# Moving a final check in front of the last products, and one row of outputs in front of the last one

## The chip, the cores and the metric

The kernel runs on one core of a Trainium2 chip. The metric is the device time of one execution in microseconds. The engines are named as the profile names them: PE is TensorE with its matrix products (PEld its weight loads), DVE is VectorE, ACT is ScalarE, POOL is GpSimd and SP is SyncE. An engine's name with a q at its end (DVEq) means its sequencer: semaphore waits, register loads and branches that never reach the engine itself.

## The reference

Routed attention is followed by a two-layer network with an ELU between its layers. A query sees only keys whose nearest centroid is the same as its own:

```python
q_assign = np.argmax(np.einsum('bhsd,hcd->bhsc', q_n, c_n), axis=-1)
k_assign = np.argmax(np.einsum('bhsd,hcd->bhsc', k_n, c_n), axis=-1)
mask = q_assign[:, :, :, None] == k_assign[:, :, None, :]
scores = scale * np.matmul(q, k.transpose(0, 1, 3, 2))
scores = np.where(mask, scores, -1000000000.0)
...
attn = attn / (np.sum(attn, axis=-1, keepdims=True) + 1e-09)
...
h = x @ w_in
g = np.where(h > 0.0, h, alpha * (np.exp(np.minimum(h, 0.0)) - 1.0))
return (g @ w_out).astype(np.float32)
```

There are 4 batches, 8 heads, 768 positions and 64 dimensions per head. The attention output, transposed, is x: 3072 tokens of 512. w_in is 512 x 2048, w_out 2048 x 512. q, k, v and the centroids are float32. The two weight matrices come as float64, and the kernel makes float32 of them during its first part, which the change doesn't touch.

## The kernel before

The work is cut into 48 attention blocks: batch, third of the queries (256 columns), pair of heads. Four of them fill one x of 512 x 256, and each x goes through the network. So there are 12 network blocks, two of them to be done when attention has ended, because the network lags seven attention blocks behind. The order of all instructions is written out by hand in one loop (`for n in range(len(blocks) + LAG)`). Each turn does one attention block, as long as there are any, and one of the four groups of a network block. Each engine takes its own instructions in that order.

A network block has four groups. The first two make the hidden layer (`hidden`, line 491 on PE, exponentials on ACT, clipping on POOL at 502, the ELU on DVE at 508). The third (`first` to `fourth`) and the fourth (`fifth` to `seventh`) make the outputs by a scheme of Strassen's kind: seven products of 8 matmuls (`product`, line 521) into two PSUM banks, `o_bank` and `f_bank`, and additions on ACT, DVE and POOL. In the two blocks behind attention PE has nothing between the products. The additions that matter here are:

- L563 (ACT) copies the third product into the second half of the temporary `ae`.
- L568 (DVE) adds the fourth product to it and writes the first half of the temporary `dt`. Fifth writes the same PSUM bank and so waits for it.
- L574 (DVE) writes the first half of the second output row tile, `o1`, from fifth.
- L581 (DVE) adds the sixth product to that and writes the second half of `o1`; L582 (POOL) then finishes the first half of `o1` with `dt`.
- L587 (DVE) adds the seventh product to the second half of `o1` and writes the second half of the first row tile, `o0`; L588 (POOL) then finishes the second half of `o1` with `ae`, and `store` (L544, on SP's queue) writes both rows of outputs, 256 KB each.

Both temporaries are called `part` in the profile, both output tiles `o_sb`.

At the end (L678 to L687) the kernel asks whether the fast path was allowed: no sum of exponentials or of their reciprocals is over a bound (`r_sum`, `d_sum`, written by ACT in each attention block), and each row has just one nearest centroid (`count`, from DVE). Seven small DVE operations make a flag for each partition (`peak`, `same`, `ok`), a product with a vector of ones adds them up on PE (L686), and a cast makes an integer of it (`go`, L687). Behind `main_path` each engine loads that integer into a register (L55) and branches on it (L56): if it is below 128, the whole computation is done again by `general_path`, and otherwise the engine jumps over that code. With these inputs every engine jumps.

The values of `r_sum`, `d_sum` and `count` are complete when the last attention block is, at n = 48 of the loop.

Of the kernel before, what the change touches and what calls it, by code (L numbers as in the profile page):

```python
# [9 lines left out]
F32 = mybir.dt.float32  # L10
# [4 lines left out]
Alu = mybir.AluOpType  # L15
Axis = mybir.AxisListType
PSUM = bass.MemoryType.PSUM

P = 128
# [6 lines left out]
R_MAX = 1e12  # L26
D_MAX = 1e15
# [33 lines left out]
def main_path(ctx, tc, c, q, k, v, centroids, moe_w_in, moe_w_out, out):  # L61
    nc = tc.nc
    B, H, S, D = q.shape
    NC = centroids.shape[1]
# [3 lines left out]
    HS = S // 2  # L68
    NQ = 3
    QS = S // NQ  # L70
# [8 lines left out]
    const = ctx.enter_context(tc.tile_pool(name="const", bufs=1))  # L79
# [11 lines left out]
    o_bank = long.tile([P, 512], F32, name="o_bank")  # L91
    f_bank = long.tile([P, 512], F32, name="f_bank")

    def banks():
        return short.tile([P, 2, 512], F32, name="banks", tag="banks")
# [13 lines left out]
    def load(name, i):  # L109
        b, pr = pairs[i]  # L110
        src = {"q": q, "k": k, "v": v}[name]
        if (name, i) in staged:
            t = first[:, ts(staged[name, i], 2 * NT * D)]
        elif name == "v":
            t = loads.tile([P, 2 * NT * D], F32, name="v_raw", tag="v", bufs=2)
        else:
            t = loads.tile([P, 2 * NT * D], F32, name=f"{name}_raw", tag="raw", bufs=4)
        if name == "v" or name == "q" and b == 0:
            t = t.rearrange("p (h t d) -> p h t d", h=2, t=NT)
            nc.sync.dma_start(  # L120
                t.rearrange("p h t d -> p h (t d)"),
                src[b, 2 * pr : 2 * pr + 2].rearrange("h (p t) d -> p h (t d)", t=NT),
            )
        elif b == 0:
            t = t.rearrange("p (t h d) -> p t h d", t=NT, h=2)
            for e in range(2):
                nc.sync.dma_start(
                    t[:, :, e], src[b, 2 * pr + e].rearrange("(p t) d -> p t d", t=NT)
                )
        else:  # L130

            for e in range(2):
                for g in range(2):
                    at = 64 * e + 32 * g
                    nc.sync.dma_start(
                        t[at : at + 32].rearrange("p (t a d) -> p t a d", t=NT, d=32),
                        src[b, 2 * pr + e, :, 32 * g : 32 * g + 32].rearrange(
                            "(a p t) d -> p t a d", a=4, t=NT
                        ),
                    )  # L140
        raw[name, i] = t
# [13 lines left out]
    ones = const.tile([P, D], F32, name="ones")  # L155
# [6 lines left out]
    for e in range(2):  # L162
# [4 lines left out]
            axis=Axis.XY,  # L167
            op=Alu.add,
# [27 lines left out]
    count = const.tile([P, 4 * B], F32, name="count")  # L196
    r_sum = const.tile([P, NQ * len(pairs)], F32, name="r_sum")
    d_sum = const.tile([P, NQ * len(pairs)], F32, name="d_sum")
# [92 lines left out]
    def w_parts():  # L291
        e_, f_ = w_out[:, : FC // 2, :QS], w_out[:, : FC // 2, QS:]
        g_, h_ = w_out[:, FC // 2 :, :QS], w_out[:, FC // 2 :, QS:]
        return e_, f_, g_, h_
# [98 lines left out]
    blocks = [(b, third, pr) for b in range(B) for third in range(NQ) for pr in range(NPR)]  # L393
# [125 lines left out]
    def product(to, left, right):  # L519
        for f in range(FC // 2):  # L520
            nc.tensor.matmul(  # L521
                to[:, :QS],
                lhsT=left[:, f],
                rhs=right[:, f],
                start=(f == 0),
                stop=(f == FC // 2 - 1),
            )

    def outer(b, third):
        half = FC // 2  # L530
        a_, c_ = g[:, :half, :P], g[:, :half, P:]
        b_, d_ = g[:, half:, :P], g[:, half:, P:]
        e_, f_, g_, h_ = w_parts()
        t1, t2, t4 = (w_sum[:, n] for n in range(3))
        seen = {}

        def temp():
            return loads.tile([P, 2, QS], F32, name="part", tag="ex", bufs=3)

        def out_tile():  # L540
            return work.tile([P, DM], F32, name="o_sb", tag="o_sb")

        def store(m, o_sb):
            nc.sync.dma_start(  # L544
                out[b * S : (b + 1) * S].rearrange("(p t) m -> p t m", t=NT)[:, QT * third + m],
                o_sb,
            )

        def first():
            product(o_bank, a_, e_)  # L550
            seen["ae"] = temp()
            nc.scalar.copy(seen["ae"][:, 0], o_bank[:, :QS])
            nc.vector.tensor_tensor(a_, g_sum, a_, op=Alu.add)

        def second():
            product(f_bank, b_, g_)
            o0, _ = seen["o"] = out_tile(), out_tile()
            nc.vector.tensor_tensor(o0[:, :QS], f_bank[:, :QS], seen["ae"][:, 0], op=Alu.add)
            nc.vector.tensor_tensor(b_, b_, g_sum, op=Alu.subtract)

        def third_():
            product(o_bank, c_, f_)
            nc.scalar.copy(seen["ae"][:, 1], o_bank[:, :QS])  # L563

        def fourth():
            product(f_bank, d_, t4)
            seen["dt"] = temp()
            nc.vector.tensor_tensor(  # L568
                seen["dt"][:, 0], f_bank[:, :QS], seen["ae"][:, 1], op=Alu.add
            )  # L570

        def fifth():
            product(f_bank, g_sum, t2)
            nc.vector.tensor_tensor(  # L574
                seen["o"][1][:, :QS], f_bank[:, :QS], seen["ae"][:, 0], op=Alu.add
            )

        def sixth():
            product(o_bank, a_, t1)
            o = seen["o"][1]  # L580
            nc.vector.tensor_tensor(o[:, QS:], o_bank[:, :QS], o[:, :QS], op=Alu.add)  # L581
            nc.gpsimd.tensor_tensor(o[:, :QS], o[:, :QS], seen["dt"][:, 0], op=Alu.add)  # L582

        def seventh():
            product(f_bank, b_, h_)
            o0, o1 = seen["o"]
            nc.vector.tensor_tensor(o0[:, QS:], f_bank[:, :QS], o1[:, QS:], op=Alu.add)  # L587
            nc.gpsimd.tensor_tensor(o1[:, QS:], o1[:, QS:], seen["ae"][:, 1], op=Alu.add)  # L588
            store(0, o0)
            store(1, o1)  # L590

        return [first, second, third_, fourth], [fifth, sixth, seventh]

    def mlp(b, third):

        steps = [lambda n=n: hidden(b, third, n) for n in range(FC // 4)]
        yield steps[:2]
        yield steps[2:] + [finish]
        yield from outer(b, third)
# [8 lines left out]
    def load_v(n):  # L608
        b, third, pr = blocks[n]
        if n not in seen:  # L610
            seen.add(n)
            load("v", b * NPR + pr)
            raw["v", n] = raw.pop(("v", b * NPR + pr))

    seen = {0}
    raw["v", 0] = raw.pop(("v", 0))
# [9 lines left out]
    for n in range(len(blocks) + LAG):  # L626
# [8 lines left out]
        if n + 1 < len(blocks):  # L635
            load_v(n + 1)
# [34 lines left out]
        for other in beside[done:]:  # L671
            if other:
                other()

    ok = c["ok"]
    peak = const.tile([P, 2], F32, name="peak")
    same = const.tile([P, 4 * B], F32, name="same")
    nc.vector.tensor_reduce(peak[:, 0:1], r_sum, axis=Axis.X, op=Alu.add)  # L678
    nc.vector.tensor_reduce(peak[:, 1:2], d_sum, axis=Axis.X, op=Alu.add)
    nc.vector.tensor_scalar(ok[:, 0:1], peak[:, 0:1], R_MAX, None, op0=Alu.is_lt)  # L680
    nc.vector.tensor_scalar(ok[:, 1:2], peak[:, 1:2], D_MAX, None, op0=Alu.is_lt)
    nc.vector.tensor_scalar(same, count, float(HS // NC), None, op0=Alu.is_equal)
    nc.vector.tensor_reduce(ok[:, 2:3], same, axis=Axis.X, op=Alu.min)
    nc.vector.tensor_reduce(ok[:, 3:4], ok[:, 0:3], axis=Axis.X, op=Alu.min)
    ps = banks()[:, 0]
    nc.tensor.matmul(ps[:1, :1], lhsT=ok[:, 3:4], rhs=ones[:, :1], start=True, stop=True)  # L686
    nc.vector.tensor_copy(c["go"], ps[:1, :1])  # L687


@with_exitstack  # L690
# [251 lines left out]
```

## Time and profile before

| what | us |
|---|---|
| median of 5 runs (1040.69 to 1043.05) | 1041.84 |
| profiled execution | 1041.97 |
| its span, first to last instruction | 1039.8 |
| around the span | 2.17 |
| PE busy | 1004.4 (97%) |
| DVE busy | 515.9 (50%) |
| ACT busy | 343.5 (33%) |
| POOL busy | 115.7 (11%) |
| mean DMA rate | 53 GB/s |

The granted clock of PE was 0.993 over the span. DVE, ACT and POOL wait for PE most of the time: their idle time costs nothing by itself. What counts is when PE waits, and what is left to do after its last product. A line of a timeline gives the start, the busy time, the engine, the line of the kernel, the operation with the tiles that it writes and reads, the shape, the number of instructions and, in brackets, how long the engine had been idle and who released it. A product of 8 matmuls shows as x16, because each float32 matmul takes two passes.

### The profile page before, as it was taken

Reading aid. Unit: us, or ns where it says so; the run is one execution under the profiler, and the core shown is the slowest. Engines: PE = TensorE matmul, PEld = TensorE weight load, DVE = VectorE, ACT = ScalarE, POOL = GpSimd, SP = SyncE. Lnnn points to the kernel's source line nnn. Section 1 sums busy time; section 2 is a strip of 40 time slices with the busy share of each in tenths; the row PEclk is TensorE's granted clock in tenths of the full one; section 3 lists DMA queues with packets and bytes.
Section 4 is the critical chain, followed back from the end, with each engine's and each line's share of the span. In section 5 each row is a group of like instructions: output and inputs, shape, how many; then the busy total and the mean of one; then the engine's idle time right before and its main releaser. Section 6 shows DMA issues by size and latency. Waiting matters only on the chain.

```text
span 1039.8 us, 14929 instructions
## 1 busy us (share of the span) xinstructions
PE 1004.4 (97%) x6403; PEld 782.2 (75%) x6403; DVE 515.9 (50%) x670; ACT 343.5 (33%) x595; POOL 115.7 (11%) x129
## 2 busy tenths in 40 slices
PE   6999989999999999999999999999999999999996
PEld 4656766777877777778778778777877877888885
DVE  4899895564343444574344246375324424423031
ACT  4676432233323332333332242234224223321010
POOL 0010121110010110111011011011011011011010
PEclk9999998999999999999999999999999999999999
DMA  9848230100122122100122103200011011000000
GB/s 274 297 121 237 63 67 19 36 16 32 36 46 48 50 45 47 51 16 16 51 45 48 39 29 56 50 26 28 16 36 31 17 36 31 16 21 1 21 1 23
DMA packets 103961, 55.60 MB, mean 53 GB/s; under 512 B 83408, under 2 KB 96720, under 8 KB 103888
## 3 DMA queue, kind: packets, MB, share of 16 engines
q1 hardware_dynamic: 103888, 54.57, 19.0%
q8 instruction: 52, 0.85, 0.3%
q14 instruction: 21, 0.17, 0.1%
HBM read 48.27 MB, written 6.29 MB: 52 GB/s over the span
## 4 chain that ended last, share of the span: by engine, by line
PE 85%; DVE 10%; ACT 3%; issue 1%; POOL 0%; DMA 0%; ACTq 0%; DVEq 0%
PE banks L491 31%; PE f_bank L521 16%; PE o_bank L521 12%; PE o_bank L452 11%; PE banks L406 9%; PE banks L441 2%; PE banks L415 2%; DVE ex L246 1%; DVE r L469 1%; DVE w_in L249 1%; ACT qm L380 1%; DVE w_in L252 1%; ACT p L423 1%; PE banks L337 1%; DVE ex L268 1%; DVE w_out L249 1%
## 5 line engine op out<-in xcount | busy, mean ns | idle before, releaser
L491 PE MATMUL banks<-xT,w_in 128*128 128x256 f32 x1536 | 338.4, 381 | 0.6 <-ACT p L423 0.3
L491 PEld LDWEIGHTS banks<-xT,w_in 128*128 128x128 f32 x1536 | 289.8, 190 | 48.2 <-issue 4.2
L406 PE MATMUL banks<-qT,kT 64*128 64x256 f32 x1152 | 166.1, 388 | 4.7 <-ACT p L423 4.7
L452 PE MATMUL o_bank<-p,v_raw 128*64 128x256 f32 x1152 | 143.8, 384 | 4.9 <-ACT p L423 4.2
L423 ACT ACTIVATE p<-banks 128x1024 f32<-128x1024 f32 x144 | 140.6, 1021 | 12.6 <-PE banks L415 11.0
L469 DVE RECIPROCAL r<-r 128x256 f32<-128x256 f32 x48 | 84.0, 1750 | 119.4 <-ACT r L468 119.3
L501 ACT ACTIVATE gT<-banks 128x1024 f32<-128x1024 f32 x48 | 49.1, 1023 | 283.9 <-PE banks L491 283.9
L508 DVE SCALAR_TENSOR_TENSOR gT<-gT,banks 128x1024 f32<-128x1024 f32 x48 | 58.4, 1216 | 155.3 <-POOL gT L502 155.2
L406 PEld LDWEIGHTS banks<-qT,kT 64*128 64x128 f32 x1152 | 87.6, 187 | 53.5 <-PE o_bank L452 10.4
L452 PEld LDWEIGHTS o_bank<-p,v_raw 128*64 128x64 f32 x1152 | 78.3, 137 | 57.6 <-issue 16.4
L521 PE MATMUL o_bank<-w_out,gT 128*128 128x256 f32 x384 | 91.1, 391 | 7.1 <-POOL w_out L302 7.1
L466 ACT COPY xT<-o_bank 128x256 f32<-128x256 f32 x48 | 17.7, 370 | 218.9 <-PE o_bank L452 218.8
L521 PEld LDWEIGHTS o_bank<-w_out,gT 128*128 128x128 f32 x384 | 73.6, 194 | 21.3 <-POOL w_out L302 8.2
L502 POOL TENSOR_SCALAR gT<-gT 128x1024 f32<-128x1024 f32 x48 | 51.1, 1066 | 342.0 <-ACT gT L501 342.0
L521 PE MATMUL f_bank<-w_out,gT 128*128 128x256 f32 x384 | 86.8, 379 | 0.0
L470 POOL TENSOR_TENSOR xT<-xT,r 128x256 f32<-128x256 f32 x48 | 39.6, 826 | 414.1 <-DVE r L469 414.1
L415 PE MATMUL banks<-qm,hot 64*128 64x256 bf16 x576 | 80.0, 269 | 2.0 <-DVE hot L366 2.0
L521 PEld LDWEIGHTS f_bank<-w_out,gT 128*128 128x128 f32 x384 | 73.0, 190 | 9.9
L429 DVE TENSOR_TENSOR psum<-p 128x1024 f32<-128x1024 f32 x38 | 47.0, 1236 | 42.5 <-ACT p L423 42.5
L380 ACT ACTIVATE qm<-hot,minus,big 64x256 bf16<-64x256 bf16 x96 | 56.7, 591 | 4.1 <-DVE hot L366 3.3
L430 DVE TENSOR_TENSOR psum<-psum,p 128x1024 f32<-128x1024 f32 x38 | 46.8, 1231 | 6.1 <-ACT p L423 2.6
L521 PE MATMUL f_bank<-w_sum,g_sum 128*128 128x256 f32 x192 | 44.6, 386 | 1.2 <-DVE part L568 1.2
(107 smaller groups left out, 773.5 us busy)
## 6 DMA issues: line engine op xcount, KB each, us to landing
v_raw<-in_v_dram SPq DMA_DIRECT2D x48, 384.0 KB, 3.2
w_sum<-in_moe_w_out_dram SPq DMA_DIRECT2D x12, 512.0 KB, 3.9
out_dram<-o_sb SPq DMA_DIRECT2D x24, 256.0 KB, 2.0
q_raw<-in_q_dram SPq DMA_DIRECT2D x48, 96.0 KB, 3.4
k_raw<-in_k_dram SPq DMA_DIRECT2D x48, 96.0 KB, 3.2
w_sum<-in_moe_w_in_dram SPq DMA_DIRECT2D x8, 512.0 KB, 7.6
w_out<-in_moe_w_in_dram SPq DMA_DIRECT2D x8, 512.0 KB, 10.3
w_out<-in_moe_w_out_dram SPq DMA_DIRECT2D x4, 512.0 KB, 4.0
```

The costliest lines, as they stand in the source:

```text
L380: nc.scalar.activation(qm[n][rows], hot[b, 0][rows, side(pr, e), ts(third, QS)], Act.Identity, scale=m, bias=minus[rows, pr % 2 : pr % 2 + 1],
L406: nc.tensor.matmul(s[:, e, ts(m, QS)], lhsT=T[i, 1][rows, ts(kt, P)], rhs=T[i, 0][rows, cols], start=True, stop=False,)
L415: nc.tensor.matmul(s[:, e, ts(m, QS)], lhsT=hot[b, 1][rows, side(pr, e), ts(kt, P)], rhs=qm[n][rows], start=False, stop=True,)
L423: nc.scalar.activation(p, s, Act.Exp, scale=SCALE)
L429: nc.vector.tensor_tensor(to, pu[n, 0], pu[n, 1], op=Alu.add)
L452: nc.tensor.matmul(o_bank[64 * e : 64 * e + 64, :QS], lhsT=raw["v", n][:, e, kt], rhs=p[:, e, ts(m, QS)], start=(kt == 0), stop=(kt == NT ...
L469: nc.vector.reciprocal(r, r)
L491: nc.tensor.matmul(hf[:, f], lhsT=w_in[:, ch, ts(4 * n + f, P)], rhs=xT[b, third][:, ch], start=(ch == 0 and f % 2 == 0), stop=(ch == KC - 1),
L501: nc.scalar.activation(t, hf, Act.Exp)
L502: nc.gpsimd.tensor_scalar(t, t, 1.0, 0.0, op0=Alu.min, op1=Alu.max)
L508: nc.vector.scalar_tensor_tensor(t, t, -1.0, hf, op0=Alu.add, op1=Alu.max)
L521: nc.tensor.matmul(to[:, :QS], lhsT=left[:, f], rhs=right[:, f], start=(f == 0), stop=(f == FC // 2 - 1),)
```

## The change

The check becomes a function, `verdict`, and is called in the turn n = 49 of the loop, behind `fourth` of the last network block but one and in front of `fifth`. Load and branch stay behind all work on each engine but SP: on SP the load of the flag stands in front of the last four stores. In all 12 network blocks, L581 writes its sum into the free half of `dt` instead of into the second half of `o1`, POOL finishes the whole of `o1` behind the sixth product (L582 and L583), and this row is stored then; the seventh product has one addition (L589) and one store behind it.

```diff
         def sixth():
             product(o_bank, a_, t1)
-            o = seen["o"][1]
-            nc.vector.tensor_tensor(o[:, QS:], o_bank[:, :QS], o[:, :QS], op=Alu.add)
+            o, u4 = seen["o"][1], seen["dt"][:, 1]
+            nc.vector.tensor_tensor(u4, o_bank[:, :QS], o[:, :QS], op=Alu.add)
             nc.gpsimd.tensor_tensor(o[:, :QS], o[:, :QS], seen["dt"][:, 0], op=Alu.add)
+            nc.gpsimd.tensor_tensor(o[:, QS:], u4, seen["ae"][:, 1], op=Alu.add)
+            store(1, o)
 
         def seventh():
             product(f_bank, b_, h_)
-            o0, o1 = seen["o"]
-            nc.vector.tensor_tensor(o0[:, QS:], f_bank[:, :QS], o1[:, QS:], op=Alu.add)
-            nc.gpsimd.tensor_tensor(o1[:, QS:], o1[:, QS:], seen["ae"][:, 1], op=Alu.add)
-            store(0, o0)
-            store(1, o1)
+            o = seen["o"][0]
+            nc.vector.tensor_tensor(o[:, QS:], f_bank[:, :QS], seen["dt"][:, 1], op=Alu.add)
+            store(0, o)
...
+    def verdict():
+
+        ok = c["ok"]
+        peak = const.tile([P, 2], F32, name="peak")
+        same = const.tile([P, 4 * B], F32, name="same")
+        nc.vector.tensor_reduce(peak[:, 0:1], r_sum, axis=Axis.X, op=Alu.add)
+        nc.vector.tensor_reduce(peak[:, 1:2], d_sum, axis=Axis.X, op=Alu.add)
+        nc.vector.tensor_scalar(ok[:, 0:1], peak[:, 0:1], R_MAX, None, op0=Alu.is_lt)
+        nc.vector.tensor_scalar(ok[:, 1:2], peak[:, 1:2], D_MAX, None, op0=Alu.is_lt)
+        nc.vector.tensor_scalar(same, count, float(HS // NC), None, op0=Alu.is_equal)
+        nc.vector.tensor_reduce(ok[:, 2:3], same, axis=Axis.X, op=Alu.min)
+        nc.vector.tensor_reduce(ok[:, 3:4], ok[:, 0:3], axis=Axis.X, op=Alu.min)
+        ps = banks()[:, 0]
+        nc.tensor.matmul(ps[:1, :1], lhsT=ok[:, 3:4], rhs=ones[:, :1], start=True, stop=True)
+        nc.vector.tensor_copy(c["go"], ps[:1, :1])
...
         for other in beside[done:]:
             if other:
                 other()
-
-    ok = c["ok"]
...
-    nc.vector.tensor_copy(c["go"], ps[:1, :1])
+        if n == len(blocks) + 1:
+            verdict()
```

More of the change, by code (lines that the diff above doesn't have):

```diff
@@ L673, in main_path @@
                 other()
-    ok = c["ok"]
[L676 to L687, printed above, removed]
+        if n == len(blocks) + 1:
+            verdict()
 @with_exitstack
```

## The prediction

> **What bounds the kernel now.** I read the page first. TensorE (PE) is busy in nearly every slice, and the chain that ended last runs 85% through it:
>
> ```profile
> PE   6999989999999999999999999999999999999996
> ...
> PE 85%; DVE 10%; ACT 3%; issue 1%; POOL 0%; DMA 0%; ACTq 0%; DVEq 0%
> ```
>
> So an edit pays only where PE waits, or behind PE's last product, and a new wait of PE costs its full length. Second, the chain's last pieces in order of time (start, length, what):
>
> ```profile
> 1028.20 3.47 PE f_bank L521 x16
> 1031.67 0.02 issue
> 1031.69 0.42 DVE o_sb L587
> ...
> 1032.52 0.50 DVE same L682
> ...
> 1033.25 0.17 DVE ok L684
> ...
> 1033.55 0.20 PE banks L686 x2
> ...
> 1033.78 0.15 DVE go L687
> ```
>
> The last product ends at 1031.67 and the span at 1039.8, so the tail is 8.13 us. Its first 2.3 us are the check. The rest stands in the answers for lines 55 and 56 (minimum/median/maximum ns, first and last start), which the chain leaves out:
>
> ```profile
> L55 DVEq TENSOR_LOAD <-go x1: 639/639/639, 1034.0 to 1034.0; - x1
> ...
> L56 DVEq COMPARE_BRANCH  x1: 72/72/72, 1034.7 to 1034.7; - x1
> L56 PEldq COMPARE_BRANCH  x1: 3458/3458/3458, 1034.7 to 1034.7; - x1
> ...
> L56 ACTq EVENT_SEMAPHORE  x1: 17/17/17, 1038.1 to 1038.1; - x1
> ...
> L56 DVEq EVENT_SEMAPHORE  x1: 21/21/21, 1038.8 to 1038.8; - x1
> ```
>
> Each engine loads the flag (0.64 us) and jumps over the general path. POOL and SP go on within 0.5 us; PE's branch lasts 3.46, ACT resumes 3.45 after its branch, DVE 4.0 after. DVE is last, and 1.0 us of barrier follows. That jump is most of the tail, and the diff leaves it: the built program has the general path between branch and target as before, whatever the words "out of line" promise.
>
> Third, the timeline where the check will stand, between fourth and fifth of the last block but one:
>
> ```profile
> 967.89 0.42 DVE L568 TENSOR_TENSOR part<-f_bank,part 128x256 f32<-128x256 f32 x1 [5.36 <-PE f_bank L521]
> 968.37 3.32 PEld L521 LDWEIGHTS f_bank<-w_sum,g_sum 128*128 128x128 f32 x16 [0.99 <-DVE part L568]
> ...
> 976.15 0.72 POOL L582 TENSOR_TENSOR o_sb<-o_sb,part 128x256 f32<-128x256 f32 x1 [20.00 <-issue]
> ...
> 1032.26 0.72 POOL L588 TENSOR_TENSOR o_sb<-o_sb,part 128x256 f32<-128x256 f32 x1 [2.74 <-DVE peak L678]
> ...
> 1032.44 0.57 DVE L682 TENSOR_SCALAR same<-count 128x16 f32<-128x16 f32 x1
> 1033.05 0.17 DVE L683 TENSOR_REDUCE ok<-same 128x1 f32<-128x16 f32 x1
> ```
>
> PE already waits there for L568, and no attention is left to fill the gap.
>
> **The change part by part.** *Stores, all 12 blocks: 0.* DVE keeps two additions of 0.42 (L581 now writes `part`). POOL's L588 (0.73) becomes L583, right behind L582 (0.72) instead of behind the last addition; one store moves forward with it. POOL stood idle 2.68 before L588 in the block at 916, and its next job (L470) came at 921.76, so L583 runs in idle time. On SP the store of the second row is issued some 2 us earlier, the other when its addition ends, as now (0.36 per issue); loads of v behind them wait for PE. L582 gets one more DMA wait, on a store one block old (landing takes 2.0): 0 to 0.05. Without the cover L583 could delay L470 by 0.73. In the tail the last store no longer waits for L588 (now issued at 1033.0, landing 1035.0); SP waits for DVE until 1038.8 anyway, so this alone is worth nothing. What it does take away is POOL's work beside the check.
>
> *Check moved: PE loses 1.06.* The built order puts seven DVE operations behind L568, then the 1x1 product on PE ahead of fifth. Now L587 starts at 1031.69 and the 1x1 weights load at 1033.52: 1.83 for an addition and the seven. L682 is 0.57 there, against 0.17 for L683 on the same 16 columns, and it ends as POOL's L588 ends (1032.26+0.72); the additions at L304 also take 3.24 instead of 1.22 beside POOL's L302. Around 968 POOL is idle from 956 to 976, so I take 0.17: 1.83-0.40 = 1.43. Its two weight loads keep PE's loader 0.11. Fifth starts 0.48 after L568 now (968.37-967.89), so the stall is 1.43+0.11-0.48 = 1.06. If L682 stays slow it is 1.46; if only the first weight load has to wait, 0.95. PE has no other gap up to 1020.5, so everything behind is late by this. Queued behind the check: on DVE the cast (waits for the 1x1 product, 0.37 now) and L574, which waits 3.8 for fifth anyway; on SP flag load and assertion (0.62+0.19+0.03) ahead of the last four stores, the first of which comes 9 us later.
>
> *Tail: 2.25 gained, perhaps 2.8.* ACT's last work is at 1017, so it loads and jumps then. PE issues ahead of its array. DVE decides: its last addition waits for the last product, and load and branch are queued behind it. A sequencer instruction follows the release of the one ahead of it, not its end: the wait before L574 is taken at 1020.6 while L568 runs from 1020.55 to 1020.97. So the load starts 0.05 behind the addition, at 1031.74 by the present clock, against 1034.0: 2.26. If it has to wait for the addition's end, 1.81. DVE's 4.0 is spent beside ACT's and PE's jumps; with ACT gone it may be ACT's 3.45. I take the middle, 0.28: 2.53. What is late next: the last store, issued 0.47 behind the product (the first of the pair now, at 1032.14), landing 2.0 later, then SP's waits (1035.5 to 1036.4, where its 2.5 of waiting for DVE begins) and the barrier; that is ready before DVE.
>
> May the load pass the waiting addition? The row: the wait ahead of the last L582 needs a store that landed 20 us before, yet starts at 1007.7, when POOL's L502 ahead of it is released (1007.77), and not after the L502 of 1000.86:
>
> ```profile
> L582 POOLq EVENT_SEMAPHORE  x11: 8654/8656/20978, 259.6 to 1007.7; - x11
> ```
>
> So a waiting instruction holds what stands behind it. The Trainium skill says otherwise ("Perfetto Trace Analysis", section "DVE / Act Engine Instruction"): an instruction goes into a wait queue and the sequencer is free at once. By the page the jump would be under way while the last product runs, and the sum would be the second rival's 1038.9, against 1040.4 by the row. I keep to the row, though it shows a semaphore wait, not a flag load.
>
> *Sum.* 2.53-1.06 = 1.47 less. The profiled execution took 1041.97 (span 1039.8 and 2.17 around it), 0.13 above the median of 1041.84; from the median 1040.4.
>
> **The rivals.** *Nothing at the end (no faster).* Something else holds DVE's branch back, or the jump alone grows as much as the check gave: the stall of 1.06 stays and the time is 1042.9. For it: the tail's largest part is untouched. Against it: nothing in the trace stands behind the last addition but load and branch.
>
> *The jump is hidden (faster).* Load and branch run while the addition still waits. Then the stores end it: 0.47 to issue, 2.0 to land, some 0.7 of SP's waits behind it, 1.0 of barrier = 4.17 behind the product, against 8.13: 3.96-1.06 = 2.90 less, 1038.9. Against it stands the POOL row; for it, that this row is of another engine and kind.
>
> *The check drags on (slower).* It decides if the stall exceeds 2.53. Should all seven operations cost what L682 does (0.61 from its start to the next's), PE would wait 0.34+7*0.61+0.12+0.11-0.48 = 4.36: 1.83 more, 1043.7. Against it: POOL idle there, and even beside POOL the operations L680 and L681 start only 0.11 and 0.07 ahead of the next.
>
> **How the numbers follow.** Chances: forecast 0.55, hidden jump 0.25, nothing at the end 0.12, dragging check 0.08. The forecast's own bounds are 1.81-1.46 = 0.35 and 2.26+0.55-0.95 = 1.86 less: 1040.0 to 1041.5. The range reaches down past the hidden jump by 0.2 for the spread of runs (1040.69 to 1043.05 over five), and up past the forecast's upper end by 0.7: 1038.7 to 1042.2; it leaves out the dragging check and most of the "nothing" case. A measurement of this kernel tells about 0.2%, 2.1 us, from no change. The forecast lies inside that but for a tenth (0.05 of 0.55), as does "nothing"; the hidden jump lies beyond it; the dragging check is counted as slower. So faster 0.30, same 0.62, slower 0.08.
>
> **What would show it.** Right: before fifth at about 968 PE waits of 1.6 together instead of 0.59 and a `same` operation of 0.17; the last product ending about 1.06 later; DVE's flag load 0.05 behind its last addition; DVE's wait at line 56 within 4.9 of it; a tail of 5.6 to 5.9; L583 right behind L582 with no PE wait near it. Wrong: DVE's load before the last addition (hidden jump); a tail still near 8; `same` at 0.57 with POOL idle; new PE waits in the eleven other blocks.

## The result, and the profile after

The changed kernel takes 1039.87 us (median of 25 runs, 1038.02 to 1041.29), the kernel before 1041.96 (46 runs, 1039.86 to 1044.14). The ratio is 0.9979, 95% interval 0.9974 to 0.9985: 2.1 us faster, 1.6 to 2.7. The prediction said 1040.4 and "within 0.2%" as the likeliest; the measured 0.21% lies on the edge of that, and the time 0.1 below the forecast's own bounds of 1040.0 to 1041.5.

Spans of single executions can't be compared for so little. The addition L568 of the last block but one begins at 967.89 in the profile before and 968.86 in the one after, and between 966.24 and 968.92 in the other profiles below, though nothing that precedes it has changed much; the difference is there already at the first L568 (166.9 to 169.6). From that addition to the last product the executions agree to some hundredths wherever PE has the same work, so each profile is read from there: 71.90 us to the end before, 70.43 after, 1.47 less.

The timeline of the changed kernel where the check now stands (start, length, engine, line, operation, and in brackets the idle time before it and who ended it):

```profile
968.86 0.42 DVE L568 TENSOR_TENSOR part<-f_bank,part 128x256 f32<-128x256 f32 x1 [5.36 <-PE f_bank L521]
...
969.61 0.17 DVE L624 TENSOR_SCALAR same<-count 128x16 f32<-128x16 f32 x1
969.80 0.17 DVE L625 TENSOR_REDUCE ok<-same 128x1 f32<-128x16 f32 x1
...
970.22 0.09 PEld L628 LDWEIGHTS banks<-ones,ok 128*1 128x1 f32 x2 [1.87 <-DVE ok L626]
...
970.34 3.32 PEld L521 LDWEIGHTS f_bank<-w_sum,g_sum 128*128 128x128 f32 x16
```

Fifth starts 1.48 behind L568, where it was 0.48: PE loses 1.00 (the prediction said 1.06). The operation on the 16 counts takes 0.17 now that POOL is idle beside it.

The chain's last pieces after, and the answers for the flag load and the branch:

```profile
1030.17 3.47 PE f_bank L521 x16
1033.64 0.02 issue
1033.66 0.42 DVE o_sb L589
```

```profile
L55 PEldq TENSOR_LOAD <-go x1: 489/489/489, 1029.6 to 1029.6; - x1
L55 POOLq TENSOR_LOAD <-go x1: 502/502/502, 1030.8 to 1030.8; - x1
L55 DVEq TENSOR_LOAD <-go x1: 545/545/545, 1033.7 to 1033.7; - x1
...
L56 SPq EVENT_SEMAPHORE  x8: 17/17/17, 1035.0 to 1037.9; - x8
...
L56 PEldq EVENT_SEMAPHORE  x1: 51/51/51, 1034.0 to 1034.0; - x1
L56 DVEq COMPARE_BRANCH  x1: 72/72/72, 1034.3 to 1034.3; - x1
...
L56 DVEq EVENT_SEMAPHORE  x1: 21/21/21, 1037.8 to 1037.8; - x1
```

The last product ends at 1033.64 and the span at 1039.3: a tail of 5.66 instead of 8.13. DVE's flag load starts with its last addition (1033.66 and 1033.7), so the wait of that addition holds it back, and nothing else does. PE loaded its flag 4 us ahead. DVE goes on 3.4 behind its branch, as ACT did before, and not 4.0.

One thing is new. SP's eight waits for the stores ran from 1035.5 to 1036.0 before; now they run to 1037.9. Before:

```profile
L56 SPq EVENT_SEMAPHORE  x8: 17/17/17, 1035.5 to 1036.0; - x8
```

The reason is the last store. The answer for the output tile, cut to the last two stores, before and after (us from issue to landing):

```profile
DMA to landing us min/median/max: 2.0/2.0/2.1
```

```profile
DMA to landing us min/median/max: 2.1/2.8/3.6
```

The last store is issued 0.49 behind the product and lands 3.6 later. DVE goes on at nearly the same time, but the waits of SP's queue tell which of the two ends the kernel. Before, SP stood 2.5 us waiting for DVE; after, it has no such wait, and its longest in the tail, 2.4, is for the last store (the view puts it down to SP's own line):

```profile
SPq L938 <- DVEq L56: 2.5, 1, 2.5
```

```profile
SPq L56 <- SPq L56: 2.9, 2, 2.4
```

From SP's last wait for a store (1037.9) to the end of the span it is 1.35; from DVE, where DVE is last, 1.0 (1038.8 to 1039.8 before). So the store alone ends this execution, 0.5 later than DVE would have.

### The profile page after: what moved, and what is told of

Same layout as the page of the kernel before. It is cut to its first block, busy times and chain, and to the rows that moved or that the text cites. A ratio compares the mean times of both kernels' runs of the same rounds, so it can differ in the third digit from the quotient of the medians.

```text
span 1039.3 us, 14929 instructions
## 1 busy us (share of the span) xinstructions
PE 1006.2 (97%) x6403; PEld 782.9 (75%) x6403; DVE 515.5 (50%) x670; ACT 343.8 (33%) x595; POOL 115.4 (11%) x129
## 4 chain that ended last, share of the span: by engine, by line
PE 85%; DVE 10%; ACT 3%; issue 1%; POOL 0%; DMA 0%; ACTq 0%; DVEq 0%
PE banks L491 31%; PE f_bank L521 16%; PE o_bank L521 12%; PE o_bank L452 11%; PE banks L406 9%; PE banks L441 2%; PE banks L415 2%; DVE ex L246 1%; DVE r L469 1%; DVE w_in L249 1%; ACT qm L380 1%; DVE w_in L252 1%; ACT p L423 1%; PE banks L337 1%; PE banks L326 1%; DVE ex L268 1%
```

## The experiments

All but the run of the general path, which stands further down, with the numbers that each is read by. "Product" is the time from L568 of the last block but one to the end of the last product, "tail" what follows, "landing" the last store's time from issue to landing; the ratio is that to the kernel before.

| kernel | product | tail | sum | landing | ratio (95%) |
|---|---|---|---|---|---|
| before | 63.76 | 8.14 | 71.90 | 2.0 | |
| changed | 64.76 | 5.67 | 70.43 | 3.6 | 0.9979 (0.9974 to 0.9985) |
| check alone | 64.76 | 6.07 | 70.83 | 3.1 | 0.9984 (0.9975 to 0.9993) |
| stores alone | 63.76 | 7.83 | 71.59 | 2.0 | 0.9994 (0.9985 to 1.0003) |
| no stall | 64.08 | 5.20 | 69.27 | 2.8 | 0.9969 (0.9958 to 0.9981) |
| no jump | 64.76 | 3.55 | 68.31 | 2.0 | 0.9958 (0.9945 to 0.9972) |
| short general path | 64.08 | 5.17 | 69.25 | 3.0 | 0.9973 (0.9964 to 0.9982) |
| PE jumps late | 64.76 | 5.94 | 70.70 | 2.4 | 0.9982 (0.9973 to 0.9991) |
| one pair in the general path | 64.08 | 5.03 | 69.11 | 2.9 | 0.9971 (0.9959 to 0.9983) |
| changed, once more | 64.76 | 5.17 | 69.93 | 2.7 | |

### The check alone, the stores alone

The first is the changed kernel with these lines as they were:

```diff
         def sixth():
             product(o_bank, a_, t1)
-            o, u4 = seen["o"][1], seen["dt"][:, 1]
-            nc.vector.tensor_tensor(u4, o_bank[:, :QS], o[:, :QS], op=Alu.add)
+            o = seen["o"][1]
+            nc.vector.tensor_tensor(o[:, QS:], o_bank[:, :QS], o[:, :QS], op=Alu.add)
             nc.gpsimd.tensor_tensor(o[:, :QS], o[:, :QS], seen["dt"][:, 0], op=Alu.add)
-            nc.gpsimd.tensor_tensor(o[:, QS:], u4, seen["ae"][:, 1], op=Alu.add)
-            store(1, o)
...
```

The second is the kernel before with only those lines changed, its check at the end.

> The check is moved in front of fifth, the stores stay as they were: two stores behind the seventh product, the second behind POOL's addition. Theory (check and jump carry the gain): PE loses 1.0 before fifth; in the tail the second store is issued 1.34 us behind the last product (1033.01-1031.67 before), 0.87 later than in the changed kernel, and it ends the kernel rather than DVE's jump: 1.34+2.0 to land+0.7 of SP's waits+0.9 = 4.9 if it lands in 2.0, so DVE's jump would still set 5.7 and the kernel takes 1040.5 (1.5 less than before, like the sum for both parts); if the code fetch of the jump holds up the store as in the profile of the changed kernel (3.6 to land), 6.5 and 1041.4. Rival (the stores carry it): no gain, 1042 or, with the stall alone, 1043.

> The row of outputs is stored ahead of the last product in all 12 blocks, the check stays at the end. Theory (the stores are worth nothing but for POOL's work beside the check): the operation on the 16 counts falls from 0.57 to 0.17, the check ends 0.40 earlier, the tail is 7.7 instead of 8.13 and the kernel takes 1041.5. Rival (the stores gain in the eleven other blocks, which would be the 0.6 us that the profile's 1.47 lacks against 2.09 in the times): 1041.0 or less, with a shorter way from the first network block to the last product.

The check alone gives 1.07 of the 1.47 in the profile, and 1040.4 us. Its two stores are issued 0.49 and 1.35 behind the product and both take 3.0 to 3.1 to land, so here too the last store, and not DVE, ends the kernel: SP passes its last wait for a store at 1037.0, DVE goes on at 1036.5, and SP has no wait for DVE. The expectation had that only as its second case, and mis-sized the hold-up by 0.5.

The stores alone give 0.31, in the time 0.0006 of it with an interval that includes nothing. The way from L568 to the last product is 63.76 as before, and so is the way through the earlier blocks: from the first L568 to the one of the last block but one it is 799.36 before, 799.37 here and 799.40 in the changed kernel. The gain is in the check at the end, which no longer meets POOL and is done 0.41 earlier:

```profile
1032.67 0.17 DVE L682 TENSOR_SCALAR same<-count 128x16 f32<-128x16 f32 x1
1032.87 0.17 DVE L683 TENSOR_REDUCE ok<-same 128x1 f32<-128x16 f32 x1
```

It was 0.57 on the same data with POOL's addition beside it. (The flag load is 0.10 shorter, too, and DVE's jump 0.18 longer, 4.2 us; no run shows why.) With the check moved, the two profiles differ by another 0.40 (70.83 to 70.43): the last store is issued 0.49 behind the product instead of 1.35. What storing a row early is worth there isn't shown: a store ends both executions, its landing differs from one execution to the next by more than that, and the intervals of the times overlap.

### The stall taken away

The seven operations stay, the check's product and cast go behind fifth:

```diff
+    def total():
         ps = banks()[:, 0]
-        nc.tensor.matmul(ps[:1, :1], lhsT=ok[:, 3:4], rhs=ones[:, :1], start=True, stop=True)
+        nc.tensor.matmul(ps[:1, :1], lhsT=c["ok"][:, 3:4], rhs=ones[:, :1], start=True, stop=True)
         nc.vector.tensor_copy(c["go"], ps[:1, :1])
...
             step()
+            if n == len(blocks) + 2 and m == 0:
+                total()
```

> As the changed kernel, but the check's product and cast stand behind fifth instead of in front of it; the seven operations on DVE stay where they are. Theory (the stall of PE in front of fifth costs its full length): fifth starts 0.48 behind L568 again instead of 1.48, the product of the check costs PE 0.1 behind fifth, and the kernel is 0.9 us faster than the changed one: 1039.0, 0.28% less than before. Rival (the stall is hidden, or something else sets the end): within 0.3 us of the changed kernel.

In its timeline fifth no longer waits for the check, whose product follows later:

```profile
966.24 0.42 DVE L568 TENSOR_TENSOR part<-f_bank,part 128x256 f32<-128x256 f32 x1 [5.36 <-PE f_bank L521]
966.72 3.32 PEld L521 LDWEIGHTS f_bank<-w_sum,g_sum 128*128 128x128 f32 x16 [0.99 <-DVE part L568]
...
970.37 0.09 PEld L630 LDWEIGHTS banks<-ones,ok 128*1 128x1 f32 x2 [0.33 <-issue]
```

The gap is 0.48 again, and the way to the last product 64.08: 0.68 less than in the changed kernel, not 0.9, because the small product behind fifth costs PE 0.32 instead of 0.1. The time is 1039.29, ratio 0.9969: 3.2 us less than before, the lowest ratio here of a kernel that leaves nothing out. Against the changed kernel the intervals overlap; the profile's 0.68 is what shows the stall.

### The jump left out

The changed kernel without load, branch and general path:

```diff
-    good = nc.values_load(c["go"][0:1, 0:1], min_val=0, max_val=P)
-    with tc.If(good < P):
-        general_path(tc, c, q, k, v, moe_w_out, out)
```

> As the changed kernel, but the load of the flag, the branch and the general path behind it are left out (with these inputs the general path isn't run). Theory (load and jump on DVE and the store held up by the code fetch set the tail of 5.66): the last store ends the kernel, 0.47 to issue+2.0 to land+0.7 of SP's waits+0.9 = 4.1 behind the last product, 1.5 less: 1038.3. Rival (the store takes its 3.6 us whatever the jump does): 5.6 behind the last product, no gain, 1039.8.

The tail is 3.55 and the store lands in 2.0; the time is 1037.93. So load and jump, with the store that they hold up, still cost the changed kernel 1.6 to 2.1 us (against its two profiles). In these profiles the store is slow only where code is fetched beside it: it also landed in 2.0 before, at 1035.05, and the first packet of code moved at 1035.55. The 0.5 by which the expectation was too long are eight of SP's waits: from the landing to the end it passes four here and takes 1.0, in the kernel with one pair below twelve and 1.6.

### How far the target lies, and who holds up the store

In the first of these, work of the general path (not run with these inputs) is given from DVE to ACT and POOL, on top of the kernel without the stall:

```diff
-                        nc.vector.tensor_copy(
+                        nc.scalar.copy(
...
-            nc.vector.tensor_scalar(e, h, 0.0, None, op0=Alu.min)
-            nc.scalar.activation(e, e, Act.Exp)
-            nc.vector.scalar_tensor_tensor(
-                g[f // NT][:, f % NT], e, -1.0, h, op0=Alu.add, op1=Alu.max
-            )
+            nc.scalar.activation(e, h, Act.Relu, scale=-1.0)
+            nc.scalar.activation(e, e, Act.Exp, scale=-1.0)
+            r = work.tile([P, HS], F32, name="g_relu", tag="relu")
+            nc.scalar.activation(r, h, Act.Relu)
+            nc.gpsimd.tensor_scalar(e, e, -1.0, None, op0=Alu.add)
+            nc.gpsimd.tensor_tensor(g[f // NT][:, f % NT], e, r, op=Alu.add)
...
```

> As the kernel without the stall, and in the general path (not run with these inputs) part of DVE's work is given to ACT and POOL, so that DVE has 174 instructions between branch and target instead of 476, and ACT 637 instead of 257. POOL has 34 there and SP 107 in the changed kernel, and both go on within 0.5 us; ACT with 257 needs 3.45. Theory (an engine stalls if the target lies too far behind the branch, and ACT's stall doesn't count, as it jumps 14 us earlier): DVE goes on 0.5 us behind its branch, the last store ends the kernel, tail 4.1 behind the last product if the store lands in 2.0, up to 5 if PE's code fetch holds it up; 0.2 to 1.1 less than the kernel without the stall: 1038.2 to 1039.1. Rival (any jump on DVE costs 3.4 to 4): tail 5.2, same time as the kernel without the stall.

Here the rival was right. DVE, 174 instructions from its target, is as slow as with 476, and POOL, now 163 from its own, has become slow too, 1.8 behind its last addition (which ends at 1030.3):

```profile
L56 POOLq COMPARE_BRANCH  x1: 45/45/45, 1029.5 to 1029.5; - x1
...
L56 POOLq EVENT_SEMAPHORE  x1: 17/17/17, 1032.1 to 1032.1; - x1
...
L56 DVEq COMPARE_BRANCH  x1: 72/72/72, 1032.4 to 1032.4; - x1
...
L56 DVEq EVENT_SEMAPHORE  x1: 21/21/21, 1035.9 to 1035.9; - x1
```

That left two readings: 174 is still too far, or DVE is slow at any distance. The next kernel calls the general path's attention for one pair of heads instead of four and so leaves out three quarters of it, which these inputs don't run:

```diff
-                    rhs=xT[half, ch],
+                    rhs=xT[half, 0],
...
-        for pr in range(NPR):
-            pair(b, pr, xT)
+        pair(b, 0, xT)
```

> As the kernel with the short general path, and the general path (not run with these inputs) leaves out three of the four pairs of heads, so that 84 instructions of DVE lie between branch and target instead of 174, 123 of POOL instead of 163, and 473 of PE. There DVE still went on 3.4 us behind its branch, and POOL, with 163, 2.6 instead of the 0.9 it needed for its own work. Theory (a target some 100 instructions on is reached at once, one of 160 or more is not): DVE goes on 0.1 to 0.5 behind its branch and is done before the store; the last store ends the kernel, tail 4.1 behind the last product if it lands in 2.0, up to 5.0 if PE's code fetch holds it up as in the last runs; 1038.2 to 1039.0. Rival (DVE's jump costs 3.4 at any distance): tail 5.2, 1039.3.

```profile
L56 DVEq COMPARE_BRANCH  x1: 72/72/72, 1033.7 to 1033.7; - x1
L56 DVEq EVENT_SEMAPHORE  x1: 21/21/21, 1034.3 to 1034.3; - x1
```

With 84 instructions between, DVE goes on 0.5 behind its branch. The price depends on the distance, and by a step: 174 and 476 cost the same 3.4. The distances are counts from the built programs. Whether it is the distance itself or where the target lies among the fetched packets of code, no run separates. Yet the time is the same as before that (1039.4, over the 1038.2 to 1039.0 that was expected), because the store took 2.9 to land and now ends the kernel alone, 1.8 us after SP began to wait for it. The two limits of the tail lie so close that taking one away gives 0.14 in the profile.

Who holds up the store was asked by making PE jump late, with one more product that reads DVE's last addition and whose result isn't used:

```diff
+    ps = banks()[:, 0]
+    nc.tensor.matmul(ps[:1, :1], lhsT=rows[-1][:, DM - 1 :], rhs=ones[:, :1], start=True, stop=True)
```

> As the changed kernel, with one more 1x1 product on PE (its result isn't used) that reads what DVE's last addition wrote, so that PE loads the flag and jumps about 0.6 behind the last product instead of 3.4 ahead of its end. Theory (the last store of the changed kernel takes 3.6 us to land instead of 2.0 because PE fetches its code at that moment): the store lands in 2.0 to 2.1 again; PE now jumps as late as DVE and goes on about 4.6 behind the last product, so the tail is 5.5 to 5.8 and the time that of the changed kernel within 0.5 us. Rival (DVE's jump, or the store's own place, holds it up): it still lands in 3 us or more.

The store lands in 2.4 instead of 3.6 (2.0 to 2.1 was expected) and PE goes on at 1038.6, 4.9 behind the last product, and ends the kernel in DVE's place: tail 5.94, time 1040.43. The DMA packets of the traces say what moved. Queue q8 carries packets of code of 16 KB and is PE's: its packets move with PE's jump. In the changed kernel one comes inside PE's branch, at 1031.64, and the next at 1034.71, 0.7 behind that jump and 0.6 behind the issue of the last store. The instruction queues from that issue to the landing, 3.59 us:

```profile
q8 instruction: 1, 0.02, 2.6%
q14 instruction: 2, 0.02, 1.3%
```

The share of q8 is 1.5 us of one of the 16 DMA engines. Of the 16 parts in which the store reports its landing, 14 came by 2.03 us, as ever, the next at 2.43 and the last at 3.59. In six profiles such a packet of PE's starts 0.2 to 0.6 behind the issue of a store of the tail, and the longer the packet took, the later that store landed, but for two packets that differ by a hundredth:

| kernel | PE's packet took | the store landed in |
|---|---|---|
| changed, once more | 0.93 | 2.66 |
| no stall | 0.97 | 2.76 |
| short general path | 1.19 | 2.98 |
| one pair in the general path | 1.20 | 2.94 |
| check alone (first of its two stores) | 1.26 | 2.99 |
| changed | 1.51 | 3.59 |

With PE late, the packet comes 1.8 behind the issue, when the store is nearly through. So most of the hold-up comes with the packet that PE fetches behind its jump, and not with the jump itself. What remains of it (0.4) no run separates: PE's late packet and two of 8 KB fall into the end of that store.

The last run is the changed kernel again.

> The changed kernel once more, for a second profile. Theory (how long the last store is held up depends on how its packets meet the code fetch, so it differs between executions): from L568 of the last block but one to the last product 64.8 as before, the store lands anywhere between 2.0 and 3.6 us after its issue, and the tail is 5.2 (DVE's jump alone) to 5.7. Rival (the store's delay belongs to the kernel): 3.6 and 5.67 again.

The store lands in 2.7 this time and SP waits for DVE again, which sets the end:

```profile
SPq L942 <- DVEq L56: 0.5, 1, 0.5
```

That is 69.93 from L568, 1.97 less than before. How long the store is held up differs from execution to execution. That the unprofiled runs gain 2.1 and the first profile 1.47 fits with this; with two profiles it isn't shown.

The general path of the short version was also made to run, by setting the bound on the sums below zero; main and general path together take 3358.26 us.

> As the kernel with the short general path, but the bound on the sums is set below zero, so that every engine falls through the branch and the general path is run after the main one. No theory is tested by its time, which is the sum of both paths, more than twice the time before; it shows what the moved operations give when they run.

It also shows the branch where it is not taken. On PE it lasted 3.56 in the same kernel with the jump, and here:

```profile
L56 PEldq COMPARE_BRANCH  x1: 95/95/95, 1029.7 to 1029.7; - x1
```

DVE goes on 0.05 behind its own. So the price is that of the jump, not of the comparison.

## Why the prediction was right, and where not

- *The stall before fifth: right.* 1.06 was said, 1.00 measured, with `same` at 0.17 as said. The 1.46 at the upper end of its bracket stood for the case that `same` stays slow without POOL beside it; the stores-alone run shows too that it doesn't.
- *The flag load behind the waiting addition: right.* On DVE it starts 0.01 to 0.02 behind the start of the last addition in every profile with the check moved, never before it. The row of POOL's semaphore wait held for a flag load on DVE. The queue rule of the Trainium skill ("Perfetto Trace Analysis", section "DVE / Act Engine Instruction") did not: by it the time would have been 1038.9, the rival at 0.25. Where nothing waits, a sequencer does run ahead: PE's load came 4.0 ahead of the last product's end, POOL's at 1030.8 ahead of its last addition at 1031.45.
- *The jump: the term was mis-sized.* The middle between DVE's 4.0 and ACT's 3.45 was taken, and without ACT's jump beside it DVE took 3.4, also where PE jumps beside it (PE late); ACT itself, jumping 14 us earlier, took 2.5. The flag load shrank from 0.64 to 0.54, which no step had and no run explains. The better end of the bracket for the tail was 2.8 of gain, and with the shorter load 2.9; the second profile of the changed kernel shows 2.97, the sum said 2.53.
- *What is late next: this step failed.* "That is ready before DVE" priced the landing at the 2.0 of a trace in which no code was fetched until the stores had landed. With the jumps earlier, code fetch and store meet: the store lands in 2.7 to 3.6. In the first profile it ends the kernel and gives back 0.5 of the gain, and it is why a cheap jump on DVE gained only 0.14.
- *The stores at nothing: right for the eleven blocks that aren't last, and alone but for the check's 0.31.* With the check moved they are not shown to be worth nothing: the last store, issued 0.86 earlier through them, ended the first profile.
- *The sum, and luck:* the first profile gives 1.47, as was said, but errors cancel there, which is luck: jump and load were 0.44 cheaper than their terms and the stall 0.06, and the late store, which had no term, took 0.5 back. The second profile, without that loss, gives 1.97, and the times 2.1. The sign "a tail of 5.6 to 5.9" came true in the first profile by the same luck; in the second the tail is 5.17. The forecast's steps up to DVE's jump are those that the runs show; the sum for them was 0.5 too low, nearly all of it from load and jump.
- *"Within 0.2%":* 2.1 was measured and 2.1 was the bound, which cuts through the interval.
- *The rivals:* "nothing at the end" is refuted by the flag load's place and the tail of 5.66 or less, "the jump is hidden" by the flag load behind the addition, "the check drags on" by `same` at 0.17 and the stall of 1.00.

That a code fetch lies behind the jump's price is supported by its dependence on distance, by the branch that isn't taken, and by the packets that the pages of the profiles count on the instruction queues. Those of the smaller engines are of 8 KB, on q14: 16 without a jump, 20 where only ACT's jump is slow among these engines (one pair), 21 with ACT's and DVE's (changed), 22 with POOL's too (short general path): among these three, one more for each further engine that pays. PE's q8 has 50 packets without a jump and 52 with. That an engine stands still until its packet is there is inferred; no row names the packet as what it waits for. The Trainium skill has the mechanism ("Runtime: NRT & Kernel Launch", section "Instruction fetch mechanics"): a taken branch out of the window that is loaded has to wait for a fetch. It gives that window as 512 instructions for most engines. The runs differ there: 163 and 174 already paid, 84 and 107 went on within 0.5, and over 123 (POOL, in the kernel with one pair) any wait hid behind POOL's last addition, 0.8 after the branch. So the measurement decides for a window of far less.

## What to carry to other kernels

A final check costs its own length and the branch behind it; both can leave the tail only on engines whose last work is early, so look for the engine that works last and ask what its sequencer still has to do. When a wait is moved to another place, move the small product too: the seven vector operations in front of fifth were free, only PE's product behind them cost 1.0, and putting it one product later gave back 0.7. When several things end a kernel within half a microsecond of each other (here a jump and a store), taking one away is worth only the distance to the next. And where a prediction and one profile agree to the hundredth, a second profile tells whether errors cancelled.

## What was not expected of the hardware

A store of 256 KB that lands in 2.0 us took 2.4 to 3.6 when code was fetched in that moment: beside a single packet of 16 KB the last of its 16 parts came up to 1.5 us late, and by another amount in each execution. On the smaller engines a jump over 84 or 107 instructions cost some 0.5 us, over 174 and more 2.4 to 4.2. POOL, which went on 0.4 behind its branch before, went on 2.6 behind it as soon as its own part of the skipped code had grown from 34 to 163 instructions. A 1x1 product between two others cost PE's array 0.32 without any wait.
